# Window attention on one core: the masks of the own key blocks go to GpSimd or VectorE, and every engine's order is searched anew

## The chip, the cores and the metric

The kernel runs on one core of a Trainium2 chip. That core has TensorE (PE, with its weight loads shown apart as PEld), VectorE (DVE), ScalarE (ACT), GpSimd (POOL) and SyncE (SP, which issues DMAs). The metric is the device time of one execution in microseconds (us), lower is better. Line numbers (L656) are those of the kernel before.

## The reference: what is computed

The input x has 2048 tokens of 512 features in bfloat16. Four residual layers follow one another: linear attention (A), attention over a sliding window (B), A again, B again, each on a layer norm of x. All have 32 heads of 16 features.

```python
# A: linear attention
phi = lambda t: jnp.where(t > 0, t + 1, jnp.exp(t)) + 1e-6
kv = einsum("bhsd,bhse->bhde", phi(k), v);  z = einsum("bhsd->bhd", phi(k))
o = (phi(q) @ kv) / (phi(q) . z + 1e-6)
# B: window of W = 256 keys, own one included
mask = (idx[:, None] - idx[None, :] >= 0) & (idx[:, None] - idx[None, :] < W)
p = softmax(where(mask, q.k * 16**-0.5, -1e9));  o = p @ v
x = x + A(ln(x)); x = x + B(ln(x)); x = x + A(ln(x)); x = x + B(ln(x))
```

## The kernel before, in words

**Tiles.** The tokens are 16 tiles of 128. A tile of x stays in SBUF from the first load to the last store (`xres`). Within a tile the heads are eight groups of four; four feature blocks f hold 128 features each.

**Graph and table.** The kernel does not write its instruction order by hand. `Plan.build` makes a graph of 2542 steps ("ops"): each has a name, the engines on which it may run with a cost in ns (`dve`, `act`, `mm`), the function that emits it, and the steps that it depends on, found from what it reads and writes (`rd`, `wr`) and from the PSUM tiles it uses (`ps`). `place` then unpacks `TABLE`, a compressed list with three parts: the order of all 2542 steps, the engine of each, and the PSUM bank of each PSUM tile. The costs play no part any more when the table is read; they were used by the search that wrote it. `synchronise` turns dependencies across engines into semaphore waits. Each engine then runs its own steps strictly in the table's order, so a step that waits holds up all steps behind it on that engine.

**One rule of `place` about GpSimd.** The names E1, xn, mk and mf are called wide (`WIDE`). Every GpSimd step, but for a few set-up steps, also waits for the last wide DVE step that stands ahead of it in the table. Nothing holds a wide DVE step back from starting while GpSimd is at work.

**Stages.** Layer 1 (A) takes each tile through layer norm (stats, aggr, eps, pow, xn), a transpose, keys and queries with phi (E on ACT, E1 and phi on DVE), and the sum over the tokens. `middle(2)` is layer 2 (B) with the end of layer 1 (`a_out`) ahead of each tile and the beginning of layer 3 (`norm`, `a_k`, `a_v`) behind it. `barrier` finishes a linear layer (den, rec, spread, pqd). `middle(3)` is layer 4 with the end of layer 3 ahead of it, and the output behind.

**The window layers around the change.** `b_scores` (L623 on) takes one key tile j, one half b of its key blocks and two feature blocks. PE computes the scores of these keys against the following 256 queries into four PSUM banks (L638), and ACT makes the exponential of two banks at a time into the buffer P (`ex`, L648). In the 64 nearest queries, those of the block's own keys, half of the scores have to be zeroed: that is the mask `mk` (L654 to L658), 128 partitions by 512 elements, done in place as a product with a triangle of ones and zeros (`tri`) on DVE (L656). In layer 4 this part is done in another way for the tiles 0 to 13 (`merged`, masks of L700); there `b_scores` returns before the mask. So 72 masks come from L656: 64 of layer 2 and 8 of the last two tiles of layer 4. `b_far` makes the scores at the window's far edge (L677, L680, exponential L690) and masks them with `mf`: the table gives a step of it either to GpSimd as an affine_select (L708) or to DVE as a product (L709), 128 by 1024. `b_values` (`pv`, L729) multiplies the probabilities with the values, and reads P once ex, mk and mf are done; rcp (L740) and div (L741) on DVE follow, then the transpose by DMA and `bout`, and the residual (L574).

Copies out of PSUM may run on ACT or DVE, as the table says: bqe, bve, ve (L395), bke (L591, L592), recb (L548). The small norm step eps (L369) may run on GpSimd or DVE; pow (L370) is always on GpSimd, and xn (L371) on DVE waits for it.

Of the kernel before, what the change touches and what calls it, by code (L numbers as in the profile page):

```python
# [218 lines left out]
def bass_view(x, free):  # L219

    return bass.AP(x.tensor, x.offset, [x.ap[0]] + free)


class Plan:
# [398 lines left out]
    def b_scores(self, j, b, fs, key):  # L623

        K = self
        ps = [Tile(1, "S") for _ in range(4)]
# [15 lines left out]
        sl = j % self.rp  # L642
# [8 lines left out]
        if skip:  # L651
            return

        def mk(e):  # L654
            x = bass_view(K.P(sl)[:, fs[0], 0, 384 * b:384 * b + 64], [[704, 4 * n], [1, 64]])
            return e.tensor_tensor(x, x, K.tri[:, 0, :].unsqueeze(1).to_broadcast([P, 4 * n, 64]), ALU.mult)  # L656
# [200 lines left out]


TABLE = (
    r"c-qZa1K1|VvaT*P*0yciwr$(CZQHhO+qTW@CcDXcb7%hV<eVfoo0F4!@AKUGhSk+o?^{*fGyMUCh3765goc+c9E6835CI|rLPAiG2oggihztY|-3#}`C",  # L860
    r"4r=n43a|>hzijl3kWoa6p#`avO+fK1uY;ujD@Ez2SkS$&>LDpE9e8oAQe1v8a6_D$N)JZ7i0tjaUd=@c<fq38+hjCLu%LreIXx=gZ!`=YC|392gRX3jE",
    r"8s-6Ba;xXbbJY!USjp?I9C9aCKn-420Zp80tY9=m1@zK6Hc3&>dnyIY<i)AUHIJK`<CP!bC^_O<)o%ghj9zmcUi$1Y4j7Y=t3k1dhTn*aop79W;b4Py#",
    r"x`WOxo!U?>cOGEf$#LQi-BFJUPxgXItmuE7^L4%guZOoQoA9lpZPumWzvN{Fjw!EBfV!=XHU2d|(4Y=<4N6L!H|m;p0kHSC5}a023~lW+<^DHU4HgD@(",
    r"-N}%?_Ew~MLpedY&Gw>S1syz@+B~;(TS-1;7z#BLZ;Z=H72~d$@RTG*)26YbZ!F?D3BViO&1yK*+Eo4-gR3epF{Rlrn1Qk(5QUz5ZRaj+KSyU3G)k84K",
    r"s>rH{DypKWf=~#mKvb1fy@O;bxpFGH8VzHhw#urqsbVU-%Aty@5~`$%rgEyvkW!^kxl}1tTIE({RaI3@l~Gkx0jQ($KwhY;>Zt~*vZ}6XsFtdgYOQLjT",
    r"B^QU18ZR&6ow*D6xyhUs;z3I8mo4yiE6K!tBTN6HB&9rde{Ip-~#M}{cr#}sDm(CjZq=s5j=*uYM!bFW7Rk{QjJm<VVxSU)~iEM5+<mLYQDMzlhgur85",
    r"XJ|s-xPVp1@O>tlq;1n4)H=nQE3=q&BL>YKfYvrm5+wlez+%)Mm9`9aRU^QuPcvt1fDeI;OU$t?Hm!sk*9<uu9c})vBB7u0FvswOj?m;J8A~R=3n~6#|",
    r"2);OdSl1t-)=bxQS6Au$wQRoB#QbzN;!C9ouZhSMs9I;;+<N9wUEh1*p~6-t%H&=>}HsGaJGx~ZaL42+4-)C<*9mBF&OOYK(A)jf4zmBTZtmkNt})LB&",
    r";o~m=|fm)+3sEg{nTB~AX0!)Mn@uez{XYirAq-tU<ysK`gI2aG(Vr@K&=WrCB#|wB7M`IEkgYj{nN`|RaYV}UNS0B_H^-;Z5KdPTpQcR8^AsnVr;V}Y^",
    r"#c?<uBVt;W0uy5etcaDcGVWE8FeRo_bulug!i*RN>){oZ2`{S&I1w9Q6|9Q&F*9bt)OZPF;bp9Y)$o&QhAnV5&cV6Z96zf`_(gqHKP$jS*ch{7Hq4GW@",  # L870
    r"Gf4#?^Hv)hxf4wHpN#;AtK>xH5q?UQ*bJ_!mHQ@b7E_}hS#y2`d;-`jOA5Zte`5YN-7Q3z+9LXJ7X8@iVH9uw#0>)8@pk5%z$|?FXlr*jZrZ_7QjUq4H",
    r"u(9i%YNv&PRvKuqRH#7-}h|$CxUX>V*YyIZnqJ7+b|rE3go*!mYRsx8n|6iG5UGRUOyhIxLL+)Bx2RS7U!w1jEr<T#rSu7>1_^R2(BxB#KP)@EJbG7kC",
    r"4A;x62cd+-N*gEz4<RiU?d3m@SVe29;+5B9~ExEG^PRLY~OQa_AFc~yTLfcaE@)ebx0U7CdhaS%Sm0_q;M$4)pHhv1JGpAt|)x=#buAoU%-#u?NRXJR#",
    r"~PBo||?Zf@}3OC?Jyn_dDCVj%sIEyyn_qYXXQ40EkUvW0gp`Q^bB`HEmMX4zX#iH1hjN;Hx9ENGAHXX#Il$?g+2poy&XfAEW=oEuuQhjPb4=@8A!ozq3",
    r"(^5{#MYpjbJ)lhVkXlkkBFas9s1+rmN0gqJgftz+%(Rl)QXLwsT2mWpPl@RmKBgzMidIuQ>Oeo?dwhrSs4mr`yp)gf(+4a-9jOU5rB2kD3X-9&)Sa5qa",
    r"Xf(^@g#Pm=G2eYQGc38mK+76`LuxI(kVQR184&Ur$RK4TF`nbOkHRb^`IgYf{Icx8bpI>Ej^_nw3&v|7Ro|dX)6_{5>%2F(jr<+*=PxEqwTbmcF;1~NF",
    r"gZ{4N)W1P?eoRQy3~mKhPT*uHMoxwTpIB4%$PBI58*Tq@0Y`P-!YdWhpF`qsCO8l5+~~NiV4vrQ~NcjC#{|G@M4zNE$_r=oRgw*R-Gd&~y5p4$~2OL8I",
    r"v?9is#EiN4Sp9z$bkFYTnYypEgmJNiuTX&il}7Tl5#Q7S%8<LLyQq!08n0r&M@8mH(qt>?^~g@2-~oSJ{6kJO4=a~md3!)aNVIRuB~P@IF?a!wA-nhz3",
    r"kE<QtN=^UM>c07S5QXUS&VR;fwrYV$;^Ko7d$KkmM=jIEvfs1i|UQX$`D6gOl{3HLw@3=h|;6i+nE>UsL#+RuqZ{$rJfy;4cF3%OXAQ$G%+?Ts>f9}9t",
    r"xg!tcPW+xfa7C`fmH7%);eI@T2lF5v!iF7ZXUh>e5@+OK9GRnVRlZ8s=sNY_o*b2X@fIG*qj)Ms<7w1~qw{E<PJ4MD-=O^*gM0HwF2SF;6lda?e3Pnib",  # L880
    r"*{lRxg_u4ojjC>@h%R|lejcb=2~2v4{>*%!ee+Uf9B!5mACN--p;q^HXY_V+>MX$F+Ra{`3u+Mqdbj|b1aU{cPI`|=aYPnm0aK%tR*hbWRzK4hU0ld-~",
    r"gZJQ+$SvSUJtt`37I);1WXWa{~@34f!UY<=cFV@9<qd$WB5_SZT!fcs7TTIoz1%@;v^^;pIL@lwk5RXOrwQmO&!Od|to{c^v1EP_l@da8n-7&G-R7<VX",
    r"CNpKxS}BCVvgw2`B7iKEIfxy*YwJ}2Ob99?$vaY@LFc>*utrTj!#u5b*ACXwW+h=h|ka*gB4Q+~$FcsZ}&n37+f^9z0^&!wPT<=7HW;!6TaD7oZ?6p%!",
# [28 lines left out]
    r">)9B5eMJ&`0bUV+w%x`2>XMr!T06JrrJkjPJ+;OkQj~KIr)i%D+#~3yRm~#Rf<`sN!vYWWCgb9~y74uwQY%#M5&l=&=rzk`EUHaDo&>z@Q1B3j`~WSPz",
    r"<)Rj;-JI0M-Y<k71@Bka|hf9sp_1LX7ajT30)f%bj)femCl0L3$)#IN)~<bsMo1ynpHKt5BCngopf(%-9Yp+H&wQbqw4FXj>yNxvbG_dvx53c>%r58~m",
    r"o353`;?j_e-P5EOdsC4|g2-JH}jrj2f4u}KA?mG@B!as5vK<&$X%RcS^ngHM+oFKn|3>===@9qssZ*K5kzW)W1)-nY",
)


# [153 lines left out]
```

## Time and profile before

| | before |
|---|---|
| time, median of 3 runs (lowest to highest) | 410.37 us (410.02 to 410.41) |
| span of the profiled execution, first to last instruction | 408.2 us |
| time beyond the span (median less span) | 2.2 us |
| instructions | 18082 |
| granted TensorE clock | 1.000 |
| first and last exponential of layer 2 | 62.7 and 224.4 us |
| first and last exponential of layer 4 | 257.6 and 400.7 us |
| masks of L656 | 72, on DVE |
| far masks | 39 on GpSimd (L708), 17 on DVE (L709) |

The time of the profiled execution itself is not listed apart from its span; the median less the span stands for what lies around it. How to read the profile: "busy" is the time in which at least one instruction of an engine is in progress, and a row's mean is the time of one instruction from start to end. Matmuls, and to a smaller degree ACT's and DVE's instructions, overlap their neighbours on the same engine, so the distance from one start to the next is shorter than the mean. `x68` counts instructions. "idle before" is time in which the engine stood still ahead of these instructions, and the arrow names what ended it. In the chain of waits the profile goes back from the last instruction to what released it.

### The profile page before, as it was taken

The page shows a single profiled execution, that of the slowest core. Times are in us where ns is not written, and L with a number is a line of the kernel's source. Part 1 is how long each engine was busy: PE and PEld are TensorE (multiplying, and loading weights), DVE is VectorE, ACT ScalarE, POOL GpSimd, SP SyncE. Part 2 cuts the span into 40 slices and gives each one's busy share as a digit, 9 for nine tenths or more (in the row PEclk, how much of TensorE's full clock was granted, in tenths as well). Part 3 has the DMA queues.
Part 4 walks back from the last instruction along what each step waited for, and adds up shares of the span by engine and source line. Part 5 has one row for each costly group of instructions (what it writes and reads, how often), then busy time and mean ns, then how long its engine had stood idle before and what let it go on. Part 6 is the DMA issues. An engine that isn't in the chain of part 4 may idle for free.

```text
span 408.2 us, 18082 instructions
## 1 busy us (share of the span) xinstructions
PE 396.0 (97%) x7997; PEld 263.4 (65%) x7997; DVE 347.9 (85%) x808; ACT 344.4 (84%) x443; POOL 113.8 (28%) x194
## 2 busy tenths in 40 slices
PE   8999999999999999999999999999999999999996
PEld 3654676666575566666666777676757766576664
DVE  5998799999998999888977789988898778876685
ACT  3655579999999999999998355999998999999992
POOL 3553632112253343330503202122123201302212
PEclk9999999999999999999999999999999999999999
DMA  8754014923242934344231100364225542442543
GB/s 247 243 118 104 2 42 121 184 56 97 65 119 52 132 73 108 75 104 106 62 69 36 29 2 28 89 127 78 71 76 130 143 83 61 66 121 62 118 109 104
DMA packets 67654, 37.88 MB, mean 93 GB/s; under 512 B 48248, under 2 KB 62712, under 8 KB 67576
## 3 DMA queue, kind: packets, MB, share of 16 engines
q1 hardware_dynamic: 67184, 35.67, 38.1%
q8 instruction: 63, 1.03, 1.1%
q0 software_dynamic: 384, 1.05, 0.8%
q14 instruction: 15, 0.12, 0.1%
q10 hardware_dynamic: 8, 0.00, 0.0%
HBM read 6.29 MB, written 2.10 MB: 21 GB/s over the span
## 4 chain that ended last, share of the span: by engine, by line
PE 81%; ACT 10%; DVE 7%; DMA 1%; issue 1%; DVEq 0%
PE ps L406 27%; PE ps L420 20%; PE ps L729 15%; PE ps L638 8%; ACT pb L648 7%; PE ps L680 2%; PE ps L481 2%; ACT pb L690 1%; DVE XQ L563 1%; PE ps L677 1%; DMA XQ<-vp 1%; PE ps L984 1%; PE ps L457 1%; PE ps L543 1%; PE ps L268 1%
## 5 line engine op out<-in xcount | busy, mean ns | idle before, releaser
L648 ACT ACTIVATE pb<-ps 128x1024 bf16<-128x1024 f32 (+3 forms) x224 | 198.2, 966 | 7.4 <-PE ps L638 6.2
L729 PEld LDWEIGHTS ps<-vB,pb 128*128 128x128 bf16 x2560 | 77.6, 96 | 11.5 <-issue 4.2
L729 PE MATMUL ps<-vB,pb 128*128 128x34 bf16 x2560 | 83.2, 177 | 0.3
L420 PE MATMUL ps<-xT,wBp 128*128 128x128 bf16 x1024 | 68.6, 219 | 0.1
L420 PEld LDWEIGHTS ps<-xT,wBp 128*128 128x128 bf16 x1024 | 58.4, 98 | 9.6 <-issue 4.0
L708 POOL TENSOR_SCALAR_AFFINE_SELECT pb<-pb 128x1024 bf16<-128x1024 bf16 x34 | 39.1, 1149 | 84.0 <-DVE pb L700 31.9
L429 ACT ACTIVATE tE<-ps 128x512 bf16<-128x512 f32 x64 | 38.1, 606 | 18.4 <-PE ps L406 12.1
L638 PE MATMUL ps<-XQ,kB 32*128 32x256 bf16 (+2 forms) x1024 | 48.7, 262 | 3.3 <-ACT pb L648 0.6
L574 DVE TENSOR_TENSOR xres<-ps,xres 128x512 bf16<-128x512 f32 x63 | 43.1, 685 | 9.6 <-PE ps L406 9.1
L690 ACT ACTIVATE pb<-ps 128x1024 bf16<-128x1024 f32 x50 | 49.0, 1048 | 1.3 <-PE ps L680 1.0
L406 PE MATMUL ps<-wA,XQ 128*128 128x512 bf16 x192 | 49.2, 380 | 0.7 <-DMA XQ<-vp 0.6
L369 POOL TENSOR_SCALAR ve<-mv 128x1 f32<-128x1 f32 x49 | 11.8, 240 | 127.9 <-DVE mv L368 126.9
L370 POOL TENSOR_TENSOR rs<-ve,negh 128x1 f32<-128x1 f32 x64 | 37.9, 592 | 32.0 <-DVE ve L369 27.5
L367 DVE BATCH_NORM_STATS2 stats<-xres 128x6 f32<-128x512 bf16 x64 | 43.8, 685 | 2.8 <-DMA xres<-in_A_x_dram 2.1
L638 PEld LDWEIGHTS ps<-XQ,kB 32*128 32x128 bf16 x1024 | 15.7, 92 | 31.4 <-ACT pb L648 8.3
L420 PE MATMUL ps<-XQ,wA 128*128 128x128 bf16 x512 | 34.4, 219 | 0.0
L406 PE MATMUL ps<-wBv,xT 128*128 128x512 bf16 x128 | 34.3, 380 | 0.0
L406 PE MATMUL ps<-M,XQ 128*128 128x512 bf16 x128 | 33.3, 380 | 0.2
L420 PEld LDWEIGHTS ps<-XQ,wA 128*128 128x128 bf16 x512 | 30.1, 98 | 5.1 <-issue 0.6
L406 PE MATMUL ps<-wBo,oT 128*128 128x512 bf16 x124 | 32.7, 380 | 0.6 <-DVE vp L431 0.4
L656 DVE TENSOR_TENSOR pb<-pb,tri 128x512 bf16<-128x512 bf16 x68 | 27.7, 419 | 3.7 <-ACT pb L648 3.1
L741 DVE TENSOR_TENSOR o<-ps,rc 128x256 bf16<-128x256 f32 x64 | 27.0, 422 | 1.7
(114 smaller groups left out, 545.9 us busy)
## 6 DMA issues: line engine op xcount, KB each, us to landing
vB<-vS SPq DMA_DIRECT2D x64, 136.0 KB, 2.6
kB<-vp SPq DMA_DIRECT2D x64, 128.0 KB, 2.2
wA<-in_A_wqkv_dram SPq DMA_DIRECT2D x3, 512.0 KB, 5.2
xres<-in_A_x_dram SPq DMA_DIRECT2D x2, 512.0 KB, 4.8
pb<-in_B_wqkv_dram SPq DMA_DIRECT2D x1, 1024.0 KB, 6.9
out_dram<-xres POOLq DMA_DIRECT2D x8, 128.0 KB, 2.5
out_dram<-xres SPq DMA_DIRECT2D x7, 128.0 KB, 2.0
xres<-in_A_x_dram SPq DMA_DIRECT2D x3, 256.0 KB, 5.3
```

The source lines that it names most:

```text
L367: self.on("DVE", "stats", lambda e: e.bn_stats(K.stats[:, t, :], K.xres[:, t, :]), key, dve(512), rd=[("xres", t)], wr=[("stats", t)])
L370: self.pow = self.on("POOL", "pow", lambda e: e.tensor_tensor(K.rs[:, t, :], K.ve[:, t, :], K.negh[:], ALU.pow), key + 0.03, (640, 690), r ...
L406: m = e.matmul(K.ps(ps), lhs(c), rhs(c), start=c == 0, stop=c == 3)
L420: m = e.matmul(K.ps(ps)[:, f * P:(f + 1) * P], w(c, f), xT(c), start=c == 0, stop=c == 3)
L429: self.on("ACT", "E", lambda e: e.activation(K.tE[:, s, :], K.ps(ps), ACT.Exp, bias=0.0), key, act(512), wr=[("tE", s)], ps=[ps])
L574: self.on("DVE", "res", lambda e: e.tensor_tensor(K.xres[:, t, :], K.ps(po), K.xres[:, t, :], ALU.add), key, dve(512), rd=[("xres", t)], w ...
L638: m = e.matmul(K.ps(ps[gq])[:, ns * i:ns * i + ns], K.kB[rows, j % 4, 2 * f + b, :, :], K.XQ[rows, f, q:q + ns], start=True, stop=True, ti ...
L648: return e.activation(out(h, ns).rearrange("p (f g) c -> p f g c", f=n), i, ACT.Exp, bias=0.0, scale=0.25)
L656: return e.tensor_tensor(x, x, K.tri[:, 0, :].unsqueeze(1).to_broadcast([P, 4 * n, 64]), ALU.mult)
L690: return e.activation(o.rearrange("p (f g) b c -> p f g b c", g=2), i, ACT.Exp, bias=0.0, scale=0.25)
L708: return e.affine_select(out=x, in_=x, compare_op=ALU.is_ge, fill=0.0, base=-2, pattern=[[0, 16], [-2, 64]], channel_multiplier=1)
L729: m = e.matmul(K.ps(ps)[:, 34 * u:34 * u + 34], K.P((b // 2) % rp)[:, f, gq % 2 * 2 + gq // 2, o:o + P], K.vB[:, (b // 2) % 4, b % 2, r, : ...
```

## The change

The mask step gets a second form. On GpSimd it is an affine_select that keeps what lies on one side of a diagonal and fills the rest with 0; on DVE it stays the product. The graph offers both engines to it, and the table is replaced as a whole. Nothing else is edited: the `WIDE` rule, the other steps and their dependencies stay.

```diff
-        def mk(e):
+        def mk(e, eng):
             x = bass_view(K.P(sl)[:, fs[0], 0, 384 * b:384 * b + 64], [[704, 4 * n], [1, 64]])
+            if eng == "POOL":
+                return e.affine_select(out=x, in_=x, compare_op=ALU.is_ge, fill=0.0, base=1, pattern=[[0, 4 * n], [2, 64]], channel_multiplier=-1)
             return e.tensor_tensor(x, x, K.tri[:, 0, :].unsqueeze(1).to_broadcast([P, 4 * n, 64]), ALU.mult)

-        self.on("DVE", "mk", mk, key + 0.02, dve(256 * n, "2x"), rd=[("P", sl, f, b, h) for f in fs for h in range(2)] + [("tri",)], wr=[("P", sl, f, b, 2) for f in fs])
+        self.g.add("mk", {"DVE": dve(256 * n, "2x"), "POOL": (600, 660)}, mk, key + 0.02, rd=[("P", sl, f, b, h) for f in fs for h in range(2)] + [("tri",)], wr=[("P", sl, f, b, 2) for f in fs])
...
 TABLE = (
...
 )
```

Unpacked, the new table says this beside the old one (numbers of steps):

| | old table | new table |
|---|---|---|
| steps on PE / ACT / DVE / GpSimd / SP | 868 / 442 / 807 / 190 / 235 | 868 / 440 / 757 / 242 / 235 |
| masks mk (128 in all) on DVE, GpSimd | 128, 0 | 76, 52 (49 of layer 2, 3 of layer 4) |
| far masks mf on DVE, GpSimd | 17, 39 | 17, 39: 13 each way; layer 2 gives 6 net to DVE, layer 4 gives 6 net to GpSimd |
| eps on DVE, GpSimd | 15, 49 | 19, 45 |
| wide DVE steps, all | 273 | 221 |
| from the first to the last ex of layer 2, ACT | 156 ex, 21 E, 10 copies | 156 ex, 20 E, 8 copies, 1 recb |
| the same, GpSimd | 24 mf, 27 pow, 20 eps, 2 constants | 18 mf, 47 mk, 27 pow, 16 eps, 2 constants |
| the same, wide DVE steps | 113 | 71 |
| from the first to the last ex of layer 4, ACT | 156 ex, 6 E, 5 copies, 1 recb | 156 ex, 6 E, 7 copies, 2 recb |
| the same, GpSimd | 15 mf, 13 pow, 8 eps, 4 stores | 21 mf, 3 mk, 13 pow, 6 eps, 7 stores |

Of PE's 868 steps 794 stand within 3 places of where they stood in PE's order, and none moves by more than 23; 419 of the 1007 PSUM tiles get another bank. The 55 lines of packed bytes become 54.

More of the change, by code (lines that the diff above doesn't have):

```diff
@@ L864 @@
[L864 to L871, printed above, removed]
@@ L912 @@
[L912 to L914 removed]
+    r"c-qxkW1u8i(hXg;ZQHhO+qP}nwr$(CZQGpb9`~2|YG!tOwtKf1f4;2B%&NE%anCssbzf%Hd*U9uXYRQJAV7HF!T>`kP!J9TG$e#X5E{Zm1V{`?ASon+<Y3^T",
+    r"iwG}VByi9iEM$Sm5CxvP7SIyL!b_I|QbH>T4p|`^M1^P&9eP1)NCk1AH)Mx=un}^=e25G2AU?E#wvZk&z&OYWk6dbK2kjvS<bpoX7ZN~ir~_RgCiH^^P!~!<",
@@ new lines @@
+    r"e;5F1U_4BKdawx&!$g<_9iSsLg2pfq20?v@1q)#jq=in<05ZZ6=mwc!FvNy*&=9&nWmpVLU<hP}&d?n;!xq>I+u$f1gZwZVrod466?(u_I1bfeIP`?8Fb%H3",
+    r"bqEVLU>Hn?rLYXD!E;y+D_}e9fD<qiD!~hQ39n!${02AS7OaGm5EoBD0hj@w0B{xTf>}@nUc+vf4aFcHo`%(M1`uz<9f*&iF*n?Wv#<veU_yKYVQ??ZfqRf1",
+    r"??VO*i{UUlzJ+&i9x~#4_zup&10ZA+R9F!6!1wSF=0YM&jG3?y7RCrT4?aK=%#2yE2^5DBFcLHxEP_QbDJH|F&<s9;!{itdBVlB$0T#1jL5PA;u@Dr7B9IM>",
+    r"VR0;h6(Bp7#ORm<b7DCd1t~Earoh@*3aUaW91W#0H<rZ`Pz^)E7|4ZXuqsx@I#>nkVlb$O4KOcM#~N4^T4F0~jWw|ru7S0%4%%RSY>w?Q1XP6e&;r|HLu`Z_",
@@ new lines @@
+    r"-~u$prq~2K;6-SL?XV17g3GWE_QL@<2%~Wfj>T~}66fMPoR3HFC_aK8U_4I1iMS3A!2+Cw>v18D!pATf7vW<35vJf3_z5=P66}bb@EFd(rT7G9;zpc>n{W<J",
+    r"#m%@Mr(tKDj!&Tr_Q0-q0L#KbT#2i2HFm=-xD31FR$PuN@Hm!-U=*A}&@-qBKf?)}jkoY5-o{_xDqh3uSc2|gFbs|*DFmLv)3^q=;Uj#ErRXq*#89{$cVKji",
+    r"L5J`O#-yIO6Q5x(3`wCVG?j*3xEt@{9;^jt@GQQ-wfG!g;ypZv=kX?9z>8R#%Fum`MF}Vjg{4b)hR#xKdVq<jES;l-RFi7a4XjOZC?1ug^7If#(P$b&d+|J7",
+    r"pj0@P;?h&RNbxBNrN+dRjM89l3`gN<AC9B(^bvo+AF%>m#t4*@DpDm%PHFKyeuqEd1WG}bDHWxph?EY$#}62ZB2z|+LiMOVU7{;^nd;C)%0!td3ss@2RE?TZ",
@@ L915 @@
+    r"@dV)@Gy7+wJ?Xq71xy}@ASX{yPb6P@uSlYOFuwQS5_@w8WP>1TzR@@P^!?p0sb3LaQlF|1*k|Jl=XscbG=Y&I%%Z&#2TdHPQP3ch1`nC>q(=5sP~MzqlxNXF",
+    r"MI|wwlh+w4$iurS@F0^Pfugmil>e)Y@>TE?`bQsuKP&t2Q36$vAeW#79!pOuuedsZ&Sw=+B&d|+4f%w9*Z~T@i%-#0*o#qtzVwR{C~eSt4-WhPj_^kp1ycIM",
+    r"UZbFrprJsu0tkZ|%8T*(-$&=8`a_$b-t;UC94Ja4Q9xU-1%1Tudjt4Ge$@g^;eWzFVSuVX;O~Lt%KOZCH4L;)pdf+yydE(=bn$)tRDr_yACsWeK~w@=<7fI^",
+    r"5MV<38{i<y-qN4~pB#VS4|ip>SNEWsum1!58!{;",
 )
```

84 lines of the change are left out of this document (40 added, 44 removed).

## The prediction

> **What bounds the kernel now.** I read the page's busy times first, then the same by stage, cutting at the first and last exponential of each window layer (62.7, 224.4, 257.6 and 400.7 us).
>
> ```profile
> PE 396.0 (97%) x7997; PEld 263.4 (65%) x7997; DVE 347.9 (85%) x808; ACT 344.4 (84%) x443; POOL 113.8 (28%) x194
> ```
>
> ```profile
> core 0: us, PE busy (x) PEld busy (x) DVE busy (x) ACT busy (x) POOL busy (x), PEclk, DMA share, GB/s
> 0.00:62.70 62.70, 60.77 (x601) 35.93 (x602) 54.93 (x133) 34.04 (x56) 28.11 (x67) 1.00 0.45 126
> 62.70:224.40 161.70, 159.63 (x3255) 103.56 (x3256) 143.58 (x337) 157.37 (x187) 48.58 (x72) 1.00 0.43 91
> 224.40:257.60 33.20, 33.10 (x528) 24.77 (x526) 29.00 (x64) 16.52 (x30) 5.71 (x11) 1.00 0.10 26
> 257.60:400.70 143.10, 138.51 (x3539) 96.48 (x3538) 117.05 (x268) 135.66 (x169) 29.30 (x40) 1.00 0.42 94
> 400.70:408.20 7.50, 4.02 (x86) 2.64 (x82) 3.36 (x9) 0.77 (x2) 2.13 (x4) 1.00 0.41 131
> ```
>
> The reader is to see that the change's home is the second row, layer 2. There ACT is busy for 157.4 of 161.7 us and DVE for 143.6; GpSimd for 48.6. PE shows 159.6 too, but its matmuls overlap, so short stalls do not show. Whether ACT is really full there needs its spacing from start to start:
>
> ```profile
> 105.07 3.77 ACT L648 ACTIVATE pb<-ps 128x1024 bf16<-128x1024 f32 x4 [0.16 <-PE ps L638]
> 108.70 0.63 ACT L429 ACTIVATE tE<-ps 128x512 bf16<-128x512 f32 x1
> 109.18 1.99 ACT L690 ACTIVATE pb<-ps 128x1024 bf16<-128x1024 f32 x2
> ```
>
> Four exponentials and the start of the next instruction lie 108.70 - 105.07 = 3.63 us apart, 0.91 each; the 512-wide one takes 109.18 - 108.70 = 0.48. Layer 2 has 156 exponentials and 31 shorter ACT instructions between its marks: 156 x 0.91 + 31 x 0.48 = 157 us of 161.7. So **ACT sets the pace of layer 2**, with some 5 us of slack, and DVE, whose work the change takes away, does not. The chain of waits for that stretch says the same from the other side:
>
> ```profile
> by line: PE ps L406 32.7%; PE ps L420 18.0%; PE ps L729 17.5%; PE ps L638 10.3%; ACT pb L648 9.5%; PE ps L677 2.8%; DVE XQ L563 1.2%; ACT pb L690 1.1%; DVE vp L431 0.9%; DVE o L741 0.7%; DVE pb L656 0.6%; ACT tE L429 0.6%; PE ps L543 0.5%;
> ```
>
> PE and ACT hold nearly all of it; the masks (L656) hold 0.6%, all DVE lines named hold 3.4%. In the stretch of layer 4 DVE is busy for 117 of 143 us, and the masks at stake are three.
>
> **The change, part by part.**
>
> *The masks leave DVE.* These are the mask's row, and the far mask's two forms, over the whole run, and then the masks in layer 2 alone:
>
> ```profile
> L656 DVE TENSOR_TENSOR pb<-pb,tri 128x512 bf16<-128x512 bf16 x68 | 27.7, 419 | 3.7 <-ACT pb L648 3.1
> L708 POOL TENSOR_SCALAR_AFFINE_SELECT pb<-pb 128x1024 bf16<-128x1024 bf16 x34 | 39.1, 1149 | 84.0 <-DVE pb L700 31.9 <-ACT pb L690 19.1 <-DVE tE L430 14.1
> L709 DVE TENSOR_TENSOR pb<-pb,tri 128x1024 bf16<-128x1024 bf16 x16 | 11.0, 690 | 0.1
> ```
>
> ```profile
> 62.70:224.40 161.70, 25.53 (x63) 1.00 0.43 91
> ```
>
> Between the marks of layer 2, 47 masks of 63 leave: 47/63 x 25.5 = 19 us of DVE; 6 far masks come back, 6 x 0.69 = 4.1. DVE's busy time there falls from 143.6 to some 128.5, its idle time from 18 to 33 us. What of it was on the path: the mask's own share, 0.6% x 161.7 = 1.0 us, of which 47/63 is **-0.7 us**. The other DVE lines of the chain (L563, L431, L741: 2.8%, 4.5 us) stand there partly because they queue behind masks; they can gain 0 to 4.5. I take a third, **-1.5**, as DVE still has 80% of its time filled and these lines themselves do not get shorter.
>
> *The masks on GpSimd.* No row shows an affine_select of 128 by 512 with two patterns. The nearest are these:
>
> ```profile
> L328 POOL TENSOR_SCALAR_AFFINE_SELECT spread<-spread 128x512 bf16<-128x512 bf16 x4 | 3.4, 848 | 0.6
> L320 POOL TENSOR_SCALAR_AFFINE_SELECT bmask<-bmask 128x128 bf16<-128x128 bf16 x1 | 0.3, 337 | 0.1
> ```
>
> L320 and L708 have two patterns as the new form has, L328 three. A line through 128 elements at 0.337 and 1024 at 1.149 gives 0.337 + 384 x 0.000906 = 0.68 us; half of L708 gives 0.57, L328 gives 0.85. I take 0.68, and 0.57 to 0.85 as its bounds: 0.26 longer than on DVE (0.15 to 0.43). GpSimd gets 47 x 0.68 - 6 x 1.15 = 25 us more in layer 2, 48.6 to about 74 of 161.7, under half. Work it out from the Trainium skill, GPSIMD Engine Reference, section 3.1, and an estimate of 0.77 comes: it gives 1.8 cycles per element at 1.2 GHz as the best case of a tight loop, and L708's 1024 elements in 1.149 us are quicker than that, so the trace does not bear it out; by 0.77 the sum would be some 0.3 us later.
>
> How much of the 0.26 counts hangs on how early the masks are. These are rows of the waits of layer 2:
>
> ```profile
> POOL pb L708 <- ACT pb L690: 19.1, 6, 6.1
> PEld ps L729 <- DVE pb L656: 1.0, 4, 0.3
> DVE xn L371 <- POOL rs L370: 0.7, 1, 0.7
> ```
>
> Only 4 of the 63 masks made a value matmul (L729) wait, 0.25 us each; the others are hidden by other tiles' matmuls. If as many of the moved ones are short of cover, 47/63 x 4 = 3 x 0.26 = **+0.8 us**; none would be 0, and the far end is a rival below. The wait added: a mask on GpSimd waits for its exponentials, and eps, pow, mf and the stores of the output queue behind it; xn on DVE, the transpose and the next tile's projections wait for pow. The first and third rows show that this has cover today: GpSimd stood for up to 6.1 us in front of a far mask, and xn waited for pow once, for 0.7 us. I set it at 0.
>
> *The port.* DVE's wide steps and GpSimd's selects can stand in each other's way. The trace has it:
>
> ```profile
> 37.57 0.85 POOL L328 TENSOR_SCALAR_AFFINE_SELECT spread<-spread 128x512 bf16<-128x512 bf16 x1
> 37.65 0.92 DVE L430 TENSOR_SCALAR tE<-tE 128x512 bf16<-128x512 bf16 x1
> 356.12 1.15 POOL L708 TENSOR_SCALAR_AFFINE_SELECT vp<-vp 128x1024 bf16<-128x1024 bf16 x1
> 356.92 0.88 DVE L709 TENSOR_TENSOR pb<-pb,tri 128x1024 bf16<-128x1024 bf16 x1
> 157.29 1.26 POOL L708 TENSOR_SCALAR_AFFINE_SELECT pb<-pb 128x1024 bf16<-128x1024 bf16 x1 [0.85 <-DVE pb L656]
> L430 DVE TENSOR_SCALAR tE<-tE 128x512 bf16<-128x512 bf16 x64 | 18.4, 292 | 2.4 <-ACT tE L429 2.0
> ```
>
> The DVE step at 37.65 takes 0.92 us in place of 0.29, and ends 0.15 after the select that began just before it; at 356.92 a far mask takes 0.88 in place of 0.69; at 157.29 the select takes 1.26. The later one waits, and the price is what is left of the earlier one. The Trainium skill, SBUF — State Buffer, section "Who interferes with whom", says that DVE in a two-port mode, or with two inputs from SBUF, shares a port pair with GpSimd as an exclusive lock: the second to start stands still until the first is done. By that rule the trace agrees, 0.92 against 0.29.
>
> The size: GpSimd's selects would fill 47 x 0.68 + 18 x 1.15 = 53 us of layer 2, a third, and 71 wide DVE steps remain there. By chance 71 x 0.33 = 23 would be held, each for about half a select, 0.4 us: 9 us of DVE. Before, chance would give 113 x 27.6/161.7 = 19, with L708's time in layer 2 from this row:
>
> ```profile
> 62.70:224.40 161.70, 27.62 (x24) 1.00 0.43 91
> ```
>
> I take 3 of those 19 as real: the table's order steers around them. The same 3 in 19 leaves 3.6 x 0.4 = 1.4 us, a third of it on the path: **+0.5 us** (0 to 9).
>
> *ACT.* In layer 2 one E and two copies leave and one recb comes, -3 x 0.48 + 0.3 = **-1.1 us**, counted in full as ACT is the bound there. In layer 4 two copies and one recb come, +1.3 us; ACT is busy for 135.7 of 143.1 there, so I count half, **+0.6**.
>
> *The rest of the order.* Few PE steps move by more than 3 places, and in the 33.2 us between the layers (PE 33.1 busy) and in the 7.5 us of the tail the work is the same. I set 0, and 3 us to both sides, as 419 tiles change their bank and each such move makes or breaks a wait that no row of before shows.
>
> *Sum:* -0.7 - 1.5 + 0.8 + 0.5 - 1.1 + 0.6 = -1.4 us. The profiled execution's span is 408.2, and the median lies 2.2 above it: 408.2 - 1.4 + 2.2 = **409.0 us**.
>
> **The rivals.**
>
> *It is hidden anyway (0.15).* ACT and PE set the pace in layer 2, masks are 0.6% of the chain, and a changed order wins in one place what it loses in another: 410.4, within 0.8. For it: the three rows of waits. Against it: ACT's shorter list, which is sure.
>
> *Relief pays in full (0.17).* DVE's lines on the chain are late only because its queue is 89% full in layer 2. Then all 4.5 us go, the masks' whole 1.0 too, and the same in part in layer 4, whose chain is this:
>
> ```profile
> by line: PE ps L420 21.6%; PE ps L406 20.1%; PE ps L729 19.6%; PE ps L638 10.1%; ACT pb L648 9.8%; PE ps L680 6.7%; ACT pb L690 2.7%; DVE XQ L563 1.7%; DVE xres L574 1.4%; issue 1.4%; DVE vS L395 1.0%; PE ps L543 0.6%; DVE o L741 0.6%; DVE
> ```
>
> Its DVE lines make 4.7%, 6.7 us, and 9 wide steps fewer stand there; a quarter is 1.7. Then -4.5 - 1.0 - 1.7 - 1.1 + 0.6 + 0.5 = -7.2, **403.2 us**. Against it: ACT has only 5 us of slack in layer 2 to give.
>
> *Masks come late from GpSimd (0.33): slower.* One mask in each of layer 2's 16 key tiles is the last thing that its value matmuls wait for, and comes 0.26 later for its own length and another half pow later, as GpSimd works in order:
>
> ```profile
> L370 POOL TENSOR_TENSOR rs<-ve,negh 128x1 f32<-128x1 f32 x64 | 37.9, 592 | 32.0 <-DVE ve L369 27.5
> ```
>
> That is 16 x (0.26 + 0.30) = 9.0 us, half of it made up again, as PE's stalls of that size are partly swallowed ahead of an ACT that is full: +4.5. It takes the place of the +0.8: -0.7 - 1.5 + 4.5 + 0.5 - 1.1 + 0.6 = +2.3, **412.7 us**. It decides from 2.2/0.28, eight late masks, on. For it: GpSimd's load grows by half, and a select now stands 47 times more in front of pow. Against it: 59 of 63 masks are early today. The port at its full 9 us, a third to a half of it on the path, would end in the same place; it has 0.06 of the 0.33, since the order before met 3 of 19.
>
> **How the numbers follow.** Forecast 0.35, hidden 0.15, relief 0.17, late 0.33. A difference within 0.2% (0.8 us) is about what a measurement of this kernel cannot tell from none; the forecast is 0.3% below. Faster: 0.35 of the forecast, less 0.08 for its lower end within the bound, and relief: 0.27 + 0.17 and a little of "hidden", 0.46. Same: 0.15 less that little, and 0.05: 0.18. Slower: late, and 0.03 of the forecast's 3 us to the other side: 0.36. The range holds forecast and hidden, two thirds of relief and two thirds of late: 403.5 to 414.0.
>
> **What would show it.** A step is right if layer 2, first to last exponential, takes about 159 us; if L656 shows some 16 DVE masks there and affine_selects of 128 by 512 at about 0.68 us; if DVE's busy time there is near 128 and GpSimd's near 74. Waits of L729 for the new select of over 2 us, or of xn for pow of over 2 us, would speak for "late"; wide DVE steps of twice their length, more than five of them, for the port. The forecast is wrong if layer 2 keeps its 161.7 us with ACT still full, or if the time is lost or won outside it, in layer 4 or in the first 62.7 us, where the new order alone has changed something.

## The result, and the profile after

The changed kernel takes 409.14 us (median of 22 runs, 407.62 to 410.89) against 410.42 us (22 runs, 408.45 to 412.73): a ratio of 0.9963, interval 0.9948 to 0.9979. Run again beside other runs of the kernel before it gave 0.9970 (0.9948 to 0.9992), with medians of 409.57 and 410.22. The ratios come from all runs, and so differ a little from the quotient of the medians. So it is 0.2 to 0.4% faster, 0.7 to 1.5 us, nearly the 409.0 that was forecast. The way there was another one. Executions that were granted less than 0.998 of the TensorE clock took longer (4 of the 35 of before in the second series, 412.9 us on average, and 1 of the 12 of the changed kernel); without these the second series gives 0.8 us.

The spans of single executions of the changed kernel differ by up to 3 us (405.9 to 409.2), more than is at stake, so I use two profiled executions of the changed kernel: the first with a span of 408.1 us, the second with 407.7. The busy line of the first:

```profile
PE 386.1 (95%) x7922; PEld 262.9 (64%) x7997; DVE 333.4 (82%) x758; ACT 341.3 (84%) x441; POOL 151.6 (37%) x246
```

PE's lower figure tells nothing: 75 matmul records are missing from this trace. DVE gave 14.5 us away, GpSimd took 37.8. Now the busy times by stage, cut at the first and last exponential of the window layers as before; first the first execution, then the second:

```profile
0.00:62.28 62.28, 59.43 (x592) 35.16 (x601) 53.49 (x131) 32.43 (x55) 29.36 (x69) 1.00 0.50 133
62.28:223.95 161.67, 155.52 (x3193) 103.89 (x3225) 135.46 (x301) 156.16 (x186) 74.20 (x112) 1.00 0.40 89
223.95:256.86 32.91, 32.42 (x551) 24.90 (x556) 28.98 (x63) 16.07 (x30) 8.48 (x15) 1.00 0.05 14
256.86:399.86 143.00, 134.83 (x3525) 96.47 (x3550) 111.75 (x256) 135.91 (x172) 39.05 (x50) 1.00 0.40 98
399.86:408.06 8.20, 3.92 (x72) 2.51 (x70) 3.75 (x9) 0.77 (x2) 0.56 (x1) 0.96 0.28 80
```

```profile
0.00:61.14 61.14, 59.30 (x592) 35.66 (x601) 53.73 (x131) 32.12 (x55) 29.56 (x69) 1.00 0.48 136
61.14:223.57 162.43, 155.49 (x3193) 103.87 (x3225) 135.78 (x301) 156.31 (x186) 74.42 (x112) 1.00 0.41 89
223.57:256.47 32.90, 32.41 (x551) 24.90 (x556) 28.98 (x63) 16.06 (x29) 8.50 (x15) 1.00 0.05 14
256.47:399.26 142.79, 134.59 (x3524) 96.22 (x3549) 111.67 (x256) 135.75 (x172) 39.14 (x50) 1.00 0.41 98
399.26:407.70 8.44, 4.10 (x73) 2.52 (x70) 3.74 (x9) 0.77 (x3) 0.56 (x1) 1.00 0.27 78
```

The reader is to compare the second row of each with the 161.70 us of before. **Layer 2, the home of the masks, is not shorter**: 161.67 and 162.43, though DVE has 8 us less to do there, ACT 1.2 less, and GpSimd's 74 us is just what was expected. What is shorter is layer 1, by 0.5 and 1.6 us; the turn between the layers wins 0.3, and the tail loses 0.7 and 0.9. The masks' own rows:

```profile
L657 POOL TENSOR_SCALAR_AFFINE_SELECT pb<-pb 128x512 bf16<-128x512 bf16 x50 | 33.7, 674 | 45.0 <-ACT pb L648 18.1 <-DVE tE L430 8.3 <-DVE pb L658 7.7
L658 DVE TENSOR_TENSOR pb<-pb,tri 128x512 bf16<-128x512 bf16 x18 | 8.4, 474 | 1.9 <-ACT pb L648 1.9
```

A select takes 0.67 us, where the line through two neighbours had given 0.68. The products left on DVE take 0.47 in place of 0.42, a first sign of the port. The waits of layer 2 that the prediction had named:

```profile
PEld ps L731 <- POOL pb L657: 1.0, 3, 0.4
DVE xn L371 <- POOL rs L370: 1.1, 3, 0.4
```

Three masks come late for their value matmuls (L731 in this numbering), 1.0 us in all, and xn waits 1.1 us for pow. By these waits the new order hides the masks on GpSimd as well as the old one hid them on DVE.

### The profile page after: what moved, and what is told of

Read it like the earlier page. It is cut to its first block, busy times and chain, and to the rows that moved or that the text cites. A ratio compares the mean times of both kernels' runs of the same rounds, so it can differ in the third digit from the quotient of the medians.

```text
span 408.1 us, 18068 instructions
## 1 busy us (share of the span) xinstructions
PE 386.1 (95%) x7922; PEld 262.9 (64%) x7997; DVE 333.4 (82%) x758; ACT 341.3 (84%) x441; POOL 151.6 (37%) x246
## 4 chain that ended last, share of the span: by engine, by line
PE 69%; ACT 12%; DVE 9%; DMA 5%; issue 2%; SPq 1%; ACTq 0%
PE ps L406 22%; PE ps L420 18%; PE ps L731 14%; ACT pb L648 9%; PE ps L638 7%; DMA xres<-in_A_x_dram 2%; PE ps L682 2%; DMA pb<-in_B_wqkv_dram 2%; DVE stats L367 1%; DVE vp L431 1%; PE ps L679 1%; ACT vp L648 1%; PE ps L457 1%; ACT pb L692 1%; DVE o L743 1%
## 5 line engine op out<-in xcount | busy, mean ns | idle before, releaser
L648 ACT ACTIVATE pb<-ps 128x1024 bf16<-128x1024 f32 (+3 forms) x224 | 198.4, 973 | 8.1 <-PE ps L638 6.6
L731 PEld LDWEIGHTS ps<-vB,pb 128*128 128x128 bf16 x2560 | 77.7, 96 | 11.2 <-issue 5.0
L731 PE MATMUL ps<-vB,pb 128*128 128x34 bf16 x2560 | 83.1, 177 | 1.0 <-issue 0.8
L710 POOL TENSOR_SCALAR_AFFINE_SELECT pb<-pb 128x1024 bf16<-128x1024 bf16 x35 | 40.4, 1155 | 64.0 <-DVE pb L702 37.2
L429 ACT ACTIVATE tE<-ps 128x512 bf16<-128x512 f32 x64 | 37.8, 605 | 24.6 <-PE ps L406 15.0
L657 POOL TENSOR_SCALAR_AFFINE_SELECT pb<-pb 128x512 bf16<-128x512 bf16 x50 | 33.7, 674 | 45.0 <-ACT pb L648 18.1
L370 POOL TENSOR_TENSOR rs<-ve,negh 128x1 f32<-128x1 f32 x64 | 37.0, 578 | 32.1 <-DVE ve L369 27.5
L406 PE MATMUL ps<-wA,XQ 128*128 128x512 bf16 x179 | 45.9, 379 | 2.8 <-DMA XQ<-vp 0.8
L420 PE MATMUL ps<-XQ,wA 128*128 128x128 bf16 x512 | 35.4, 219 | 0.1
L369 POOL TENSOR_SCALAR ve<-mv 128x1 f32<-128x1 f32 x45 | 11.3, 252 | 63.2 <-DVE mv L368 61.1
L420 PEld LDWEIGHTS ps<-XQ,wA 128*128 128x128 bf16 x512 | 30.5, 98 | 5.9 <-issue 0.7
L742 DVE RECIPROCAL rc<-ps 128x16 f32<-128x16 f32 x64 | 16.1, 252 | 20.2 <-PE ps L731 19.7
L406 PE MATMUL ps<-wBv,xT 128*128 128x512 bf16 x108 | 30.1, 380 | 2.4 <-issue 1.3
L406 PE MATMUL ps<-wBo,oT 128*128 128x512 bf16 x103 | 28.5, 380 | 3.0 <-issue 1.8
L406 PE MATMUL ps<-M,XQ 128*128 128x512 bf16 x114 | 29.7, 380 | 1.3 <-issue 0.6
```

Of the source, the lines that this page charges most:

```text
L370: self.pow = self.on("POOL", "pow", lambda e: e.tensor_tensor(K.rs[:, t, :], K.ve[:, t, :], K.negh[:], ALU.pow), key + 0.03, (640, 690), r ...
L406: m = e.matmul(K.ps(ps), lhs(c), rhs(c), start=c == 0, stop=c == 3)
L420: m = e.matmul(K.ps(ps)[:, f * P:(f + 1) * P], w(c, f), xT(c), start=c == 0, stop=c == 3)
L429: self.on("ACT", "E", lambda e: e.activation(K.tE[:, s, :], K.ps(ps), ACT.Exp, bias=0.0), key, act(512), wr=[("tE", s)], ps=[ps])
L648: return e.activation(out(h, ns).rearrange("p (f g) c -> p f g c", f=n), i, ACT.Exp, bias=0.0, scale=0.25)
L657: return e.affine_select(out=x, in_=x, compare_op=ALU.is_ge, fill=0.0, base=1, pattern=[[0, 4 * n], [2, 64]], channel_multiplier=-1)
```

## The experiments

My theory was the sum of the prediction: layer 2 gains 2 us from a shorter ACT list and a relieved DVE. The rivals were: masks hidden anyway, relief that pays in full, masks late from GpSimd, and, from the profile after, a gain outside layer 2. All ratios are to runs of the kernel before on the same chip. This table has the stages of one profiled execution of each kernel, in us, cut at the same exponentials:

| kernel | layer 1 | layer 2 | turn | layer 4 | tail | ratio (interval) |
|---|---|---|---|---|---|---|
| before | 62.7 | 161.7 | 33.2 | 143.1 | 7.5 | 1 |
| changed, first | 62.3 | 161.7 | 32.9 | 143.0 | 8.2 | 0.9963 (0.9948 to 0.9979) |
| changed, second | 61.1 | 162.4 | 32.9 | 142.8 | 8.4 | 0.9970 (0.9948 to 0.9992) |
| masks_only | 64.0 | 166.6 | 33.2 | 143.6 | 7.5 | 1.0095 (1.0059 to 1.0132) |
| order_only | 61.9 | 183.0 | 35.7 | 142.4 | 8.6 | 1.0495 (1.0451 to 1.0538) |
| masks_twice | 62.1 | 173.9 | 34.2 | 143.2 | 8.7 | 1.0291 (1.0252 to 1.0331) |
| masks_out | 63.0 | 161.7 | 33.2 | 143.3 | 7.5 | 0.9973 (0.9950 to 0.9997) |
| masks_out_new | 61.2 | 162.0 | 32.9 | 142.2 | 8.2 | 0.9960 (0.9938 to 0.9982) |
| layer2_new | 63.3 | 162.1 | 32.9 | 143.1 | 7.5 | 1.0028 (1.0008 to 1.0049) |
| layer2_old | 61.3 | 162.2 | 33.2 | 144.2 | 8.2 | 1.0013 (0.9987 to 1.0039) |
| layer1_new | 62.1 | 164.0 | 33.2 | 143.6 | 7.6 | 0.9973 (0.9949 to 0.9997) |
| old_layer4 | 61.6 | 162.1 | 32.9 | 143.7 | 7.5 | 0.9968 (0.9943 to 0.9993) |
| wp_moved | 63.3 | 161.7 | 33.2 | 143.9 | 7.6 | 0.9997 (0.9973 to 1.0021) |
| act_longer | 62.7 | 170.4 | 33.2 | 143.3 | 7.6 | 1.0191 (1.0154 to 1.0228) |

The columns of this table say more than any single ratio. Six of the kernels have the old order up to step 405 or further (before, masks_only, masks_out, layer2_new, wp_moved, act_longer): their layer 1 takes 62.7 to 64.0 us, 63.2 on average. The eight executions with the new order there take 61.1 to 62.3, 61.7 on average. The two sets do not overlap and lie **1.5 us** apart. Layer 2 with the new order and its masks on GpSimd takes 161.7 to 162.4 us in four executions; with the old order and masks on DVE it takes 161.7, 161.7, 162.2 and 164.0. Layer 4 with the new order is some 0.7 us shorter (layer2_old left aside, for a reason given below) and the tail behind it 0.8 longer, so these two cancel.

**Is DVE's relief worth anything: masks_out.** The kernel before without the 52 masks.

```diff
     wide = None
+    gone = {481, 489, 493, 547, 551, 555, 559, 613, 617, 621, 625, 687, 745, 749, 753, 757, 811, 815, 819, 888, 892, 953, 957, 961, 1022, 1026, 1030, 1087, 1091, 1095, 1099, 1160, 1164, 1225, 1229, 1237, 1294, 1298, 1302, 1306, 1346, 1350, 1354, 1398, 1402, 1406, 1440, 1444, 1452, 2475, 2500, 2512}
+    for o in order:
+        for d in [d for d in o.deps if d.i in gone]:
+            o.deps.remove(d)
+            o.deps.extend(x for x in d.deps if x not in o.deps)
+    order = [o for o in order if o.i not in gone]
     for o in order:
```

> The kernel before, with the 52 masks left out altogether, so that the scores above the diagonal of those blocks are not zeroed; the order of all other steps is the old one. It shows the most that moving the masks can give without a new order. My own account: 2.2 us, 0.5% faster than before. If DVE relief pays in full: 5 us or more, 1.3%. If the masks are hidden: within 0.2%.

Measured: 0.9973 (0.9950 to 0.9997). Its row of layer 2, of the busy times by stage, to be held against that of before (161.70, DVE 143.58):

```profile
63.01:224.66 161.65, 159.62 (x3255) 103.61 (x3254) 128.80 (x288) 157.37 (x187) 48.70 (x72) 1.00 0.43 92
```

DVE does 14.8 us less and the stretch is the same to a few hundredths. So in layer 2 the masks are hidden, and of the relief of 2.2 us that I had counted there nothing is seen. The time's ratio lies 0.3% below 1 (0.1% by the medians, 410.27 and 410.70), with its interval close to 1 at one end and 2 us below at the other; no stage of the profile shows that gain, and whether it is one stays open. The 14.8 us for 49 masks are 0.30 each, less than the 0.42 of a mask's own record, since neighbours overlap; together with the far masks that came back, the two copies that ACT gave to DVE, and the steps held at the port, this is why DVE lost 8 us in layer 2 and not the 15 of the prediction.

**What ACT is worth there: act_longer.** The order before, with a small ACT instruction behind each exponential of layer 2.

```diff
+        first = [o for o in self.g.ops if o.name == "ex"][:156]
+        last = next(o for o in self.g.ops if o.name == "c1")
+        for k, o in enumerate(first):
+            x = Op(-1, {"ACT": 1}, lambda e: e.activation(self.idle[:], self.ident[:, 0:8], ACT.Copy), 0.0, "idle")
+            x.eng, x.t0 = "ACT", o.t0 + 0.5
+            order.append(x)
+        order.sort(key=lambda o: o.t0)
+        for x in order:
+            if x.name == "idle":
+                x.deps, last = [last], x
...
```

> The kernel before, with one idle ACT instruction (128 by 8, nobody waits for it) behind each of layer 2's 156 exponentials, some 0.06 to 0.1 us each, 9 to 16 us of ACT. If ACT sets the pace of layer 2, as I hold, with 5 us of slack: 5 to 11 us slower, 1.2 to 2.7%. If PE, or latency through several engines, sets it: under 3 us, 0.7%.

Measured: 1.0191 (1.0154 to 1.0228). From its timeline on ACT and its busy times by stage:

```profile
105.92 0.20 ACT L950 ACTIVATE idle<-ident 128x8 bf16<-128x8 bf16 x1
106.01 1.01 ACT L648 ACTIVATE pb<-ps 128x1024 bf16<-128x1024 f32 x1
```

```profile
62.72:233.15 170.43, 158.10 (x3221) 103.17 (x3254) 144.52 (x337) 169.15 (x343) 49.03 (x72) 1.00 0.39 86
```

Each idle instruction holds the next exponential back by about 0.1 us (0.098 at the median of the 156), 15 us together. Layer 2 is 8.7 us longer. What changed is seen in the chain of waits by engine, over the whole run, before and then here:

```profile
PE 81%; ACT 10%; DVE 7%; DMA 1%; issue 1%; DVEq 0%
```

```profile
PE 44%; ACT 43%; DVE 8%; issue 2%; DMA 1%; DVEq 0%
```

Cut at layer 2's exponentials, PE holds 82% of the chain before and 6% here, ACT 11% before and 88% here. So ACT sets the pace of the lengthened layer 2. That it set it in the kernel before, as I held, is not shown: there PE held the chain, and by its busy time stood still for only 2 of the 161.7 us. ACT's slack was larger, too, than I had worked out. This is the row of L648 up to the end of layer 2, before:

```profile
L648 ACT ACTIVATE pb<-ps x128: 378/1024/1130, 62.7 to 223.8; 128x1024 bf16<-128x1024 f32 x116, 128x768 bf16<-128x768 f32 x4, 128x256 bf16<-128x256 f32 x4, 128x512 bf16<-128x512 f32 x4
```

I had priced all 156 exponentials of layer 2 as if they were 1024 wide; 12 are narrower. With the shortest distance to the next start that the trace shows for each width (0.90, 0.69, 0.49 and 0.26 us, and 0.48 to 0.66 for the 31 other instructions), ACT needs some 151 us, and has 10 us of slack rather than 5. Adding 15 us must lengthen such a stretch by 4 us or more, whoever set its pace before; so this run does not tell ACT from PE there. What it does fit is that 1.2 us less on ACT brought nothing.

**The masks moved, nothing else: masks_only.**

```diff
 # table: order and banks as before; engines:
-52 of the mk: DVE
+52 of the mk: POOL
```

> The old order and banks; only the engine of the 52 masks is set to GpSimd. If the masks are hidden and cheap anyway: within 0.2% of before. My own account (mask and queue relief 2.2 us, late masks 0.8, but an order that does not steer around the port: 9 us of DVE held, a third of it on the path, 3 us): 0.3 to 0.5% slower, with DVE's wide steps stretched in many more than five places. If relief of DVE pays in full: at least 0.5% faster.

Measured: 1.0095 (1.0059 to 1.0132), slower, by twice what I expected; layer 2 is 5 us longer. From its waits, over the whole run:

```profile
DVE xn L371 <- POOL rs L370: 7.2, 9, 1.7
PE ps L731 <- POOL pb L657: 2.8, 4, 1.2
PEld ps L731 <- POOL pb L657: 2.4, 3, 1.3
```

Both slow mechanisms are there. xn waits 7.2 us for pow, which stands behind masks on GpSimd, where it waited 0.7 before. And masks come late for the value matmuls: the rows of PE and PEld count in part the same waits, a matmul's and that of its weights, so they are not to be added; taken together by their times they are 3.6 us, in place of 1.0 before. The two mechanisms make more than the 5 us lost, so neither can count in full. Of the two, I had set the first at 0.

**The new order without the move: order_only.**

```diff
 # table: order and banks as changed; engines:
-52 of the mk: POOL
+52 of the mk: DVE
```

> The new order and banks, but all masks back on DVE. If the whole gain is that of a better order, wherever the masks run: as fast as the changed kernel, 0.4% faster than before. My own account (ACT's shorter list -1.1, layer 4 +0.6, no relief): about 0.1% faster than before, so 0.2 to 0.3% slower than the changed kernel. If relief of DVE is what pays: 0.5% slower than before or more, as the order was laid out for a DVE with 16 us less to do in layer 2.

Measured: 1.0495 (1.0451 to 1.0538). The new order is no better order in itself. Its layer 2 takes 183 us, and its waits show that the masks stand wrongly in DVE's queue:

```profile
PEld ps L731 <- DVE pb L658: 10.5, 10, 2.2
DVE pb L658 <- ACT pb L648: 9.3, 11, 1.6
PE ps L731 <- DVE pb L658: 6.1, 6, 1.9
```

A mask whose exponentials are not done holds DVE for 9.3 us in all, with everything behind it, and PE waits 10.5 us for masks (both rows taken together by their times). A part of the 21 us that layer 2 is longer may come from the clock (see the last section). Order and engines of layer 2 belong together.

**How much cover the masks have: masks_twice.** The changed kernel; each mask on GpSimd is followed by the same mask again.

```diff
+        if o.name == "mk" and o.eng == "POOL":
+            x = Op(-1, o.engs, o.emit, 0.0, "mk")
+            x.eng, x.t0, x.deps = o.eng, o.t0 + 0.5, [o]
+            for c in order:
+                if o in c.deps:
+                    c.deps.append(x)
...
```

> The changed kernel, with each of the 52 masks on GpSimd made a second time in place (the second changes nothing in the values). 52 x 0.68 = 35 us more on GpSimd, and every one of these masks is done 0.7 us later or more. If the masks have cover, as I hold: 1 to 4 us slower than the changed kernel, up to 1%. If late masks already cost time (the rival on the slow side): at least 16 x 0.7 = 11 us, 2.7% slower.

Measured: 1.0291 (1.0252 to 1.0331), and 0.9970 for the changed kernel: 3.2% slower, 13 us. I had expected 1 to 4. From its waits (L741 and L667 are the value matmul and the select in its numbering):

```profile
PEld ps L741 <- POOL pb L667: 8.9, 10, 1.5
PE ps L741 <- POOL pb L667: 6.5, 10, 1.1
DVE xn L381 <- POOL rs L380: 5.6, 11, 1.8
PEld ps L741 <- POOL pb L720: 2.4, 2, 2.2
```

By their times the first two rows are 9.5 us of waiting of PE for masks, in place of 1.0. Far masks (L720) come late as well, and xn waits 5.6 us for pow, where it waited 2.4 in the changed kernel: the second copies delay everything behind them on GpSimd. So the masks' cover in the new order is thin, for a dozen of them less than what the second copies added, but the 13 us are not the price of late masks alone. My "masks are early" held for the order as it stands. By what I had written down, 3.2% spoke for masks that are late already; the next run says that they are not.

**What the masks on GpSimd still cost: masks_out_new.** The edit of masks_out, made to the changed kernel.

> The changed kernel with the 52 masks left out, so that the scores above the diagonal of those blocks are not zeroed. If the masks on GpSimd are hidden, as the old order's were: within 0.2% of the changed kernel, 0.4 to 0.5% faster than before. If they cost there what a second copy of them costs (14 us for 52): up to 14 us faster than the changed kernel, at least 4.

Measured: 0.9960 (0.9938 to 0.9982); the changed kernel beside it 0.9970 (0.9948 to 0.9992). Within 0.2%: in the new order the masks are hidden, too, but for 0.3 us by the medians (409.30 and 409.57). Their second copy costs 13 us and their first hardly anything.

**Which part of the table wins: layer2_new and layer2_old.** Both tables hold nearly the same steps in their first 435 and in their first 1662 places, so they can be joined there.

```diff
 # layer2_new: order, engines and banks
+old[:405] + new[:1662] (what is not yet there) + rest as in old
 # layer2_old
+new[:435] + old[:1662] (what is not yet there) + rest as in new
```

> The old table up to the first exponentials of layer 2 and again from the first exponential of layer 4 on; the new order, engines and banks in between, with 49 masks on GpSimd. My account as predicted puts the gain here (-0.7 - 1.5 + 0.8 + 0.5 - 1.1 = -2.0 us): 0.5% faster than before. If layer 2 is worth nothing, as its equal stretch in the two profiles (161.7 us in both) suggests: within 0.2% of before.

> The counterpart: the new table for layer 1 and from layer 4's first exponential on, the old one for layer 2 between, all its masks on DVE. My account as predicted: +0.6 us, 0.15% slower than before. If the gain comes from outside of layer 2: the whole 0.3 to 0.4% faster than before.

Measured: 1.0028 (1.0008 to 1.0049) and 1.0013 (0.9987 to 1.0039). The new layer 2 alone wins nothing and is rather slower, against my account; its counterpart is not faster either. Its layer 1 is short, 61.3 us, but its layer 4 took 144.2 us in the profiled execution. In that layer the granted TensorE clock was 0.50 for 3.4 us, from 387.9 us on, so the 144.2 is not to be read for the order. The two parts do not add up to the 0.3% of the whole: layer2_old has the short layer 1 and is not faster, and why stays open. What I can say from them is only that the new layer 2 by itself is not the gain.

**Layer 1 alone: layer1_new, and with layer 2: old_layer4.**

```diff
 # layer1_new
+new[:435] + rest as in old
 # old_layer4
+new[:1662] + rest as in old
```

> The new table for layer 1 only (its first 435 steps, up to the first exponentials of layer 2), the old one from there on; no mask on GpSimd. In the profiles so far the new order of layer 1 reaches the first exponential at 61.1 to 62.3 us, the old one at 62.7 to 64.0. If that is where the gain comes from: 1.3 us, 0.3% faster than before. As I predicted (the rest of the order at 0): within 0.2%.

> The new table up to the first exponential of layer 4 (49 masks on GpSimd), the old one behind it. The profiles so far give the old tail 0.7 us less than the new one. If gains and losses by stage add up: 0.1 to 0.2% faster than the changed kernel, 0.45% faster than before. If a lead won early is given back by the later stages' orders: no faster than the changed kernel.

Measured: 0.9973 (0.9949 to 0.9997) and 0.9968 (0.9943 to 0.9993). The new order of layer 1, without one mask on GpSimd, is as fast as the whole change within the intervals. The old tail brings nothing on top: no version that computes everything beats the changed kernel. The interval of layer1_new ends close to 1, just as that of masks_out, which I left open; alone it proves little. Its weight comes from the stage table, where all eight executions with this order of layer 1 end it earlier. The profiled execution of layer1_new was the slowest of its twelve (span 410.4, median 408.0), so its later stages are not to be read for the gain.

**What in layer 1: wp_moved.**

```diff
 # table: order and banks as before; engines of the eight wp (L355)
-ACT x6, POOL x2
+ACT x4, POOL x4
```

> The old order; only the eight copies of the query and key weights (L355) get the engines that the new table gives them (4 on GpSimd, 4 on ACT, in place of 2 and 6). In the chain of before they stand between two exponentials of layer 1 at 23.6 to 25.4 us. If they are what the new order of layer 1 gains by: the first step behind layer 1's sum over the tokens starts 1 us earlier, 0.25% faster. If it is the earlier layer norms of the last tiles: within 0.2% of before, or slower, as GpSimd has them late.

Measured: 0.9997 (0.9973 to 1.0021). Nothing that shows: the copies alone do not bring it. What differs shows in the chain of waits between 22.5 and 37 us. Before (24 pieces, the DVE part from 25.84 on shortened here):

```profile
23.01 0.60 ACT tE L429
23.60 0.66 ACT wBp L355
24.27 0.44 ACT tE L429
24.71 0.67 ACT wBp L355
25.37 0.44 ACT tE L429
...
29.91 0.32 DVE vp L371
30.23 0.34 DVE stats L367
30.57 4.23 DMA XQ<-vp
34.84 1.47 PE ps L406 x6
```

The same stretch in the second execution of the changed kernel (23 pieces, all of PE):

```profile
27.80 0.86 PE ps L481 x4
28.66 0.86 PE ps L406 x4
29.52 1.29 PE ps L481 x6
30.82 0.86 PE ps L406 x4
```

Before, the chain leaves PE at 23.0, runs through ACT and DVE's queue, and waits 4.2 us for a transposed tile; PE goes on at 34.8. What PE itself loses there is less, by its wait in the kernel before:

```profile
PEld ps L406 <- DMA XQ<-vp: 1.1, 1, 1.1
```

Its matmuls stand still for 0.6 us there, and for 0.7 to 0.9 in the other four kernels whose layer 1 is wholly of the old order (masks_only, masks_out, wp_moved, act_longer). None of the eight executions with the new order has such a stop of over 0.2 us between 22 and 47 us. The chain itself is a weaker witness. After, in this execution, PE is on it throughout; in the first execution of the changed kernel it runs through DVE and ends in a wait of 2.5 us for such a tile, and in layer2_new, whose layer 1 takes 63.3 us, it is all PE. The layer norms of the last tiles stand earlier in DVE's order, by these rows of the 16 statistics steps of layer 1, before and in that second execution:

```profile
L367 DVE BATCH_NORM_STATS2 stats<-xres x16: 660/684/696, 2.9 to 33.3; 128x6 f32<-128x512 bf16 x16
```

```profile
L367 DVE BATCH_NORM_STATS2 stats<-xres x16: 660/686/695, 2.9 to 30.5; 128x6 f32<-128x512 bf16 x16
```

The last one starts at 30.5 us in place of 33.3; over all kernels, at 30.5 to 31.7 with the new order and at 33.1 to 34.3 with the old. That the new order ends layer 1 earlier is shown by the stage table. The earlier layer norms go together with it in every execution, but were not tried by themselves, and the stop of 0.6 to 0.9 us is only about half of the 1.5.

## Why the prediction was right, and where it was not

The number and the sign were right: 409.0 against 409.14. The reasons were mostly not, and that the number fits is luck: layer 2, where the sum had put 2.0 us, gave nothing, and some 1.5 us came from layer 1, which it had set at 0. The prediction's own signs of being wrong both came: layer 2 kept its 161.7 us with ACT still busy for 156 of them, and the time was won outside it.

- *What bounds layer 2.* Not shown. That DVE does not set its pace is right (masks_out). But ACT has 10 us of slack, not 5, as 12 of its exponentials are narrower than the sum took them; and the lines of the chain that the prediction showed gave PE 82% and ACT 11%. act_longer shows only what a lengthened ACT does.
- *The relief of DVE, -0.7 and -1.5.* Wrong: nothing of it in layer 2 (masks_out: 161.65 against 161.70 us with 14.8 us of DVE's work gone). This is the step that failed: a third of the chain's DVE lines and the masks' own share were counted as path, and the stretch does not get shorter when they are served earlier. The rival "hidden anyway" described layer 2 as it is.
- *ACT's shorter list, -1.1.* ACT did lose 1.2 us of work, and layer 2 no time. I had counted it in full although the same prediction had found 5 us of slack; work that has slack is not path.
- *Layer 4, +0.6.* 143.1 became 143.0 and 142.8: ACT's longer list costs nothing there that shows.
- *Masks on GpSimd, 0.68 us and +0.8.* The length is right (0.67), GpSimd's 74 us too, and 1.0 us of waits is near the 0.8 that the step had said; as time it is 0.3 us by the medians and can hardly be told from 0 (masks_out_new). But the cover was read from the old order. With that order the move costs 0.95% (masks_only). The rival "late" is what the move is without a new order; it had put the time 2.3 us above before, where masks_only is 3.9 us above (0.95%), and it left out the wait of xn for pow.
- *The port, +0.5.* In layer 2 ten wide DVE steps were held, not 3.6, by 2.1 us in all where I had 1.4: each for less. No run prices it apart from the rest; with the stretch unchanged, nothing of it shows as time.
- *The rest of the order, 0, and 3 us to both sides.* This is where the result came from: layer 1 -0.5 and -1.6 in the two executions (-1.5 over all kernels), the turn -0.3, the tail +0.7 and +0.9. The prediction named this as what would make it wrong, "the first 62.7 us, where the new order alone has changed something".

## What to carry to other kernels

An engine that is 89% busy in a stage can still be worth nothing there: leave its work out and look at that stage's length before you count on relief. An engine's slack has to be worked out from all the widths of its instructions, and held against that engine's share of the chain of waits; here both spoke against ACT as the only bound. Where every engine runs a fixed order, a step's engine and its place are one decision; moved alone, the same masks cost 1%, and the new order without the move 5%. When a whole order is replaced, cut both orders at a place where they hold the same steps and join the halves; here these joins, and the stage lengths of all of them side by side, point to a layer that the change was not about. And rows of waits of PE and of its weight loads often count one wait twice: look at their times before adding them.

## What was not expected of the hardware

The port's price can be read step by step: in the first execution of the changed kernel 17 wide DVE steps began while a select was running, and the 13 wide steps that took over 0.04 us more than usual are all among them; before, 6 began so and 4 were stretched. The longest of the masks began 0.44 us after a far mask's select; this is GpSimd, and then DVE, by the timeline:

```profile
173.14 1.15 POOL L710 TENSOR_SCALAR_AFFINE_SELECT pb<-pb 128x1024 bf16<-128x1024 bf16 x1 [0.72 <-DVE xn L371]
```

```profile
172.98 0.68 DVE L395 CAST vp<-ps 128x512 bf16<-128x512 f32 x1
173.58 0.97 DVE L658 TENSOR_TENSOR pb<-pb,tri 128x512 bf16<-128x512 bf16 x1
```

The mask ends at 174.55, 0.26 after the select's end at 174.29, and takes 0.97 in place of 0.42. The copy out of PSUM just ahead of it ran into the same select and took its usual 0.68: of the copies at L395, 22 began during a select, and their median is 0.69 us, as for all of them.

And order_only, though PE waits more in it, was granted a lower TensorE clock in layer 2, 0.97 on average against 1.00 in the other kernels. It is not lower throughout: the trace has it at 0.50 for 3.4 us at a time, three times in layer 2 (from 88.6, 105.7 and 133.0 us on), and at 1.00 in between. By an estimate from these figures, half the clock for 10.2 us loses at most 5.1 of the 21 us. Two of these stretches begin some 2 to 4 us after long stops of PE (1.6 us from 86.0 on, 1.9 from 129.4 on), but a stop of 1.8 us from 172.9 on is followed by none; no run here says what sets them off.

```profile
61.86:244.89 183.03, 166.33 (x3226) 105.28 (x3225) 150.07 (x348) 157.85 (x186) 42.64 (x65) 0.97 0.35 79
```
